# Bringing the tokens of experts 1 to 7 into columns with VectorE squares and SBUF transfers instead of TensorE turns

## The chip, the cores and the metric

The kernel runs on one core of one Trainium2 chip. The metric is the device time of one execution in microseconds (us); the median of three runs is given. Times taken from a trace are those of one profiled execution, counted from the start of its span.

Five engines work side by side, each in the order of its own instructions: TensorE (PE; its weight loads are PEld), VectorE (DVE), ScalarE (ACT), GpSimd (POOL) and SyncE (SP). They wait for each other by semaphores. In this kernel SP issues nearly all plain transfers, and POOL issues the indirect ones (gathers and scatters by an index).

## The reference: what is computed

Threshold attention over 8 batches, 8 heads, 576 positions and head size 64, and then a mixture of 8 experts over the 4608 resulting tokens of width 512. Each token goes to one expert, chosen by its id.

```python
scores = scale * np.matmul(q, k.transpose(0, 1, 3, 2))
thresh = np.max(scores, axis=-1, keepdims=True) - tau
scores = np.where(scores >= thresh, scores, -1000000000.0)
...
attn = np.exp(scores)
attn = attn / (np.sum(attn, axis=-1, keepdims=True) + 1e-09)
return np.matmul(attn, v).astype(np.float32)
...
x = np.ascontiguousarray(attn_out.transpose(0, 2, 1, 3)).reshape(B * S, H * D)
...
expert_idx = token_ids * np.int64(2654435761) % np.int64(E)
for e in range(E):
    mask = expert_idx == e
    ...
    xe = x[mask]
    h = np.maximum(xe @ w1[e], 0.0)
    out[mask] = h @ w2[e]
```

All is float32; w1 is 512 x 1024 and w2 1024 x 512 for each expert. With the inputs of the reference the experts get 598, 596, 571, 565, 599, 533, 570 and 576 tokens.

## The kernel before, in words

**Attention.** Two heads of one batch make a pair; there are 32 pairs, and the head pair `hp` is the outer loop (8 batches for each of the 4 head pairs). A pair takes 5 steps, and the loop `for n in range(LAST + NS + 1)` (L608) is an order written out by hand: within `tc.manual_schedule()` every engine gets its instructions in the order of the text. A step makes scores (`score`, L214), negates them and takes the row maximum (`negate`, L225, on VectorE), takes exponentials (`expo`, L239, on ScalarE), masks (`mask`, L250, on VectorE, with the threshold `thr` that GpSimd computes in L232), turns the weights (`turn_w`, L261) and multiplies by v (`av_part`, L292). At the end of a pair `put_xm` (L326) scales the result (`xm`, L331, on VectorE) and SP writes it to DRAM (L337, L342). Head pairs 0 to 2 go to `xa_dram`, 384 wide, head pair 3 to `xb_dram`, 128 wide (`x_place`, L313).

**Routing.** Small VectorE operations between the steps (`route`, L345) give every token a slot: expert e has the slots e x CAP to e x CAP + CAP - 1. CAP is 610: three tiles of 128 rows and two of 113. Tokens beyond CAP go to overflow slots, which the loop at the end (L805) would process; with these counts it makes no pass. Then `scatters` (L475) sends token numbers into two tables in DRAM by 36 indirect transfers, SP reads the tables back as `gidx` and `gidx_odd` (L488, four transfers), and VectorE takes their minimum (L494).

**Gathers.** `fetch(e, kt, part)` (L109) brings the 128 rows of tile `kt` of expert `e` from `xa_dram` (part 0) or `xb_dram` (part 1) into one of ten buffers `xg_bufs`. Part 0 of experts 0 and 1 is fetched in ten steps from step G0 = 130 on, part 1 after the attention loop (L698), when the last `xb_dram` write has landed.

**Expert 0** gets its columns early: `early_xT` (L539) turns blocks of 64 x 128 on TensorE and ScalarE copies them into `xT_0`. `early_h` (L561) multiplies head pairs 0 to 2 by w1 as filler between the last attention steps, and `late_h` (L576) adds head pair 3 and applies the maximum with 0.

**Experts** (L781, also in an order by hand): for each `e`, `gemm1` (L726: 8 blocks of hidden units, 2 halves of CAP/2 columns, 4 blocks of the width; not for expert 0), the load of w1 and the ten fetches for expert e + 2, `gemm2_last` (L749) for the last two tiles together, then for the first three tiles `gemm2` (L742), with `turn_last` (L764) turning the outputs of the last two tiles back. `store` (L771) copies to SBUF on ScalarE and scatters rows to `out` on POOL. Between these stand the pieces of `turn_x` for expert e + 1: `put_xT` (L719) makes four TensorE turns of 128 x 128 for each of five tiles (L722, against the identity matrix), and VectorE copies the result from PSUM into `xT` (L724).

Of the kernel before, what the change touches and what calls it, by code (L numbers as in the profile page):

```python
# [9 lines left out]
FP32 = mybir.dt.float32  # L10
BF16 = mybir.dt.bfloat16
FP16 = mybir.dt.float16
I32 = mybir.dt.int32
# [7 lines left out]
def kernel(  # L21
# [33 lines left out]

    KT, KF, TL = 5, 3, 113
    TROWS = [P] * KF + [TL] * (KT - KF)
    FIRST = [sum(TROWS[:k]) for k in range(KT)]
    CAP = sum(TROWS)
    CH = CAP // 2  # L60
# [4 lines left out]
               for m in range(1, E + 1) if m * (CAP + 1) <= N)  # L65

    slot_dram = [nc.dram_tensor(f"slot_scratch_{i}", (NSLOT, 1), I32, kind="Internal").ap()  # L70
                 for i in range(2)]

    XA = DIN - P
    xa_dram = nc.dram_tensor("xa_scratch", (N, XA), FP32, kind="Internal").ap()
    xb_dram = nc.dram_tensor("xb_scratch", (N, P), FP32, kind="Internal").ap()

# [14 lines left out]
    keep_any = consts.tile([P, 1], FP32, name="keep_any")  # L91
    drop = consts.tile([P, 1], FP32, name="drop")
    gidx = consts.tile([P, E, KT], I32, name="gidx")
    gidx_odd = consts.tile([P, E, KT], I32, name="gidx_odd")
    ov_i = consts.tile([P, NOV + 1], I32, name="ov_i")


    xg_bufs = [consts.tile([P, DIN], FP32, name=f"xg_{i}") for i in range(2 * KT)]
    xT_0 = consts.tile([P, CO, CAP], FP32, name="xT_0")
    h_0 = consts.tile([P, FO, CAP], FP32, name="h_0")  # L100
    w_tiles = {}

    def gather(x_dram, dst, idx):
        nc.gpsimd.indirect_dma_start(
            out=dst, out_offset=None, in_=x_dram[:, :],
            in_offset=bass.IndirectOffsetOnAxis(ap=idx, axis=0),
            bounds_check=N - 1, oob_is_err=False)

    def fetch(e, kt, part):  # L109
        xg = xg_bufs[(e * KT + kt) % (2 * KT)]  # L110
        dram, dst = (xa_dram, xg[:, 0:XA]) if part == 0 else (xb_dram, xg[:, XA:DIN])
        gather(dram, dst, gidx[:, e, kt:kt + 1])

# [10 lines left out]
    with tc.tile_pool(name="a_q", bufs=1) as a_q, \  # L124
# [188 lines left out]
        def x_place(p):  # L313
            hp, b = divmod(p, B)
            return (xa_dram, b * S, hp * P) if hp < HP - 1 else (xb_dram, b * S, 0)

# [9 lines left out]
        def put_xm(p):  # L326
# [8 lines left out]
                .to_broadcast([P, NS, 2, D]), op=ALU.mult)  # L335
            x_dram, r0, c0 = x_place(p)
            nc.sync.dma_start(  # L337
# [134 lines left out]

        placed = []

        def scatters():  # L475

            for c in range(NTC):
                nc.gpsimd.indirect_dma_start(
                    out=slot_dram[c % 2][:, :],
                    out_offset=bass.IndirectOffsetOnAxis(ap=slot_i[:, c:c + 1], axis=0),  # L480
                    in_=tok[:, c:c + 1], in_offset=None, bounds_check=NSLOT - 1,
                    oob_is_err=False)
                yield
            for _ in range(4):
                yield
            for table, dst in zip(slot_dram, (gidx, gidx_odd)):
                for p0, p1, k in ((0, TL, KT), (TL, P, KF)):
                    nc.sync.dma_start(  # L488
                        out=dst[p0:p1, :, 0:k],
                        in_=bass.AP(tensor=table.tensor, offset=p0 * KT,  # L490
                                    ap=[[k, p1 - p0], [CAP, E], [1, k]]))
            for _ in range(4):
                yield
            nc.vector.tensor_tensor(out=gidx[:], in0=gidx[:], in1=gidx_odd[:], op=ALU.min)  # L494

# [30 lines left out]
        def constants():  # L526
# [6 lines left out]
            nc.gpsimd.memset(gidx[:], BIG)  # L533
            nc.gpsimd.memset(gidx_odd[:], BIG)
            nc.gpsimd.iota(tok[:], pattern=[[1, NTC]], base=0, channel_multiplier=NTC)
# [3 lines left out]
        def early_xT(tr, k0, k1, c0, c1):  # L539

            blocks = [(kt, co) for kt in range(k0, k1) for co in range(c0, c1)]
            for i, (kt, co) in enumerate(blocks):
                for r in (0, 64):
# [3 lines left out]
                                        ident[r:r1, r:r1])  # L547
            for ka, kb in ((k0, min(k1, KF)), (max(k0, KF), k1)):
                for r in (0, 64):
# [41 lines left out]
        LAST = NS * NP  # L591
        G0 = NS * ((HP - 1) * B + 2)
        pieces, scatter_pieces = route(), scatters()
        h_pieces = early_h()

# [4 lines left out]
        with tc.manual_schedule():  # L600
# [7 lines left out]
            for n in range(LAST + NS + 1):  # L608
# [11 lines left out]
                if s == 3 and n < LAST:  # L620
                    next(pieces, None)
                if s == 1 and 3 <= p < 2 + len(xg_bufs):
                    nc.sync.dma_start(out=xg_bufs[p - 2][:], in_=xg_bufs[0][:])
                q = p - 1
                if s == 1 and 0 <= q < NP:
# [66 lines left out]

                g = n - G0
                if 0 <= g < 2 * KT:
                    fetch(g // KT, g % KT, 0)
                if n == LAST:
                    fill(1)
            for g in range(2 * KT):  # L698
                fetch(g // KT, g % KT, 1)
            fill(FO * 2 * (CO - 1) - 18)  # L700
            tr = ps_tr.tile([P, 2, 512], FP32, name="tr")
            early_xT(tr, 0, KT, CO - 1, CO)
            fill(18)
            late_h()

    with tc.tile_pool(name="m_x", bufs=1) as m_x, \
# [6 lines left out]

        o_bufs = [m_o.tile([P, DIN], FP32, name=f"o_{i}") for i in range(KT)]
        oT_sb = m_o.tile([P, CO, CAP - FIRST[KF]], FP32, name="oT_sb")
        for o_sb in o_bufs:
# [47 lines left out]
        def turn_last(kt, idx):  # L764
            o_ps = ps_x.tile([P, CO, P], FP32, name="xT_ps")
            s0 = FIRST[kt] - FIRST[KF]
            for co in range(CO):
                nc.tensor.transpose(o_ps[0:TL, co, :], oT_sb[:, co, s0:s0 + TL], ident[:])
            store(o_ps[:].rearrange("p c d -> p (c d)"), kt, idx, TL)

# [6 lines left out]

        def turn_x(e, kt):
            put_xT(xg_bufs[(e * KT + kt) % (2 * KT)], xT_bufs[e % 2], kt, TROWS[kt])

        with tc.manual_schedule():  # L781
            for e in range(E):
                if e > 0:
                    gemm1(w_tiles.pop((e, 1)), xT_bufs[e % 2], h_bufs[e % 2], 2, CH)
                if e + 2 < E:
                    load_w1(e + 2)
                    for g in range(2 * KT):
                        fetch(e + 2, g // 2, g % 2)
                w2_sb = w_tiles.pop((e, 2))
                if e + 1 < E:  # L790
                    turn_x(e + 1, 0)
                    turn_x(e + 1, 1)
                gemm2_last(w2_sb, h_bufs[e % 2])
                for kt in range(KF):
                    if e + 1 < E:
                        turn_x(e + 1, kt + 2)
                    gemm2(w2_sb, h_bufs[e % 2], kt, gidx[:, e, kt:kt + 1], P)
                    if kt < KT - KF:
                        turn_last(KF + kt, gidx[:, e, KF + kt:KF + kt + 1])
                if e + 2 < E:  # L800
                    load_w2(e + 2)
# [3 lines left out]
        with tc.For_i(0, n_ov, 1) as it:  # L805
# [14 lines left out]
            nc.vector.tensor_tensor(out=idx[:], in0=idx[:], in1=idx_odd[:], op=ALU.min)  # L820
            gather(xa_dram, xg_bufs[0][:, 0:XA], idx[:, 0:1])
            gather(xb_dram, xg_bufs[0][:, XA:DIN], idx[:, 0:1])
            put_xT(xg_bufs[0], xT_0, 0, P)
# [36 lines left out]
```

## Time and profile before

| what | us |
|---|---|
| median of three runs | 1042.09 (1041.54 to 1042.26) |
| profiled execution | 1026.92 |
| its span | 1025.3 |
| mean granted TensorE clock | 0.996 |
| w x v, L292, TensorE busy | 184.0 |
| gemm1, L731, TensorE busy | 231.2 |
| gemm2, L745, TensorE busy | 168.9 |
| gemm2_last, L757, TensorE busy | 99.0 |
| thresholds, L232, POOL busy | 102.3 |
| 40 + 40 gathers, L104, POOL busy | 43.8 + 40.3 |

A line of groups names the source line, the engine and the operation, what is written and read, the shape, how often, then the busy time and the mean duration of one, and last how long the engine sat idle before it and what ended that idle time. Matmul ends are modelled and overlap the next matmul's start by a little, so two starts are a better measure of a stage than a sum of durations. A product in float32 appears as two records. A timeline line begins with a start and a duration. "SPq" is the issuing of a transfer by SP.

### The profile page before, as it was taken

How to read it: one execution, taken by the hardware profiler on the slowest of the kernel's cores; microseconds unless marked ns; L12 is line 12 of the kernel's file. 1: busy time of each engine (PE TensorE's matmuls, PEld its weight loads, DVE VectorE, ACT ScalarE, POOL GpSimd, SP SyncE). 2: the span in 40 equal slices, each digit the busy share in tenths (PEclk: the TensorE clock that was granted, in tenths of full speed). 3: DMA queues.
4: the chain of work that ended last, by engine and by line, in shares of the span. 5: the costliest groups of instructions: out<-in, count | busy, mean ns of one | idle time of the engine just before them, and what ended most of it. 6: DMA issues, size and time to landing. Idle time of an engine off the chain costs nothing. (4 is left out here: it accounts for less than half of the span.)

```text
span 1025.3 us, 20443 instructions
## 1 busy us (share of the span) xinstructions
PE 1007.2 (98%) x7752; PEld 672.2 (66%) x7752; DVE 507.1 (49%) x1353; ACT 451.8 (44%) x737; POOL 316.4 (31%) x431
## 2 busy tenths in 40 slices
PE   8999999999999999999999999999999999999995
PEld 4666666666666666666857757668577577685772
DVE  7999999999999999983300101001001010010000
ACT  5888888888888988880210010000100100101001
POOL 3233332677773356322413041050140310101001
PEclk9999999999999999999999999999999999999998
DMA  7345554445565598311313241142042412300001
GB/s 178 84 113 138 137 123 114 94 111 118 118 186 155 141 250 197 82 33 27 131 42 133 82 154 43 81 153 82 35 139 82 143 40 93 108 1 37 10 1 47
DMA packets 92146, 103.50 MB, mean 101 GB/s; under 512 B 24709, under 2 KB 65788, under 8 KB 92048
## 3 DMA queue, kind: packets, MB, share of 16 engines
q1 hardware_dynamic: 83424, 83.06, 29.9%
q0 software_dynamic: 8192, 18.91, 5.5%
q8 instruction: 63, 1.03, 0.4%
q14 instruction: 35, 0.29, 0.1%
q10 hardware_dynamic: 432, 0.21, 0.1%
HBM read 81.87 MB, written 20.01 MB: 99 GB/s over the span
## 5 line engine op out<-in xcount | busy, mean ns | idle before, releaser
L239 ACT ACTIVATE w<-ns,nmx 128x576 f32<-128x576 f32 x288 | 220.3, 776 | 34.7 <-DVE ns L225 34.6
L731 PE MATMUL sc<-xT,w_sb 128*128 128x305 f32 x896 | 231.2, 419 | 0.0
L250 DVE SCALAR_TENSOR_TENSOR w<-ns,thr,w 128x576 f32<-128x576 f32 x288 | 226.0, 817 | 0.0
L731 PEld LDWEIGHTS sc<-xT,w_sb 128*128 128x128 f32 x896 | 169.3, 189 | 63.2 <-issue 3.3
L225 DVE TENSOR_SCALAR_CACHE_REDUCE ns<-sc 128x576 f32<-128x576 f32 x288 | 205.4, 746 | 6.2 <-PE sc L214 5.5
L214 PE MATMUL sc<-k_sb,q 64*128 64x288 f32 (+1 forms) x1280 | 178.9, 423 | 1.3 <-DVE k_sb L523 0.7
L745 PE MATMUL o_ps<-w_sb,h 128*128 128x512 f32 x384 | 168.9, 593 | 0.0
L774 POOL DMA_INDIRECT out_dram<-o,gidx x40 | 39.5, 987 | 409.0 <-ACT o L773 350.8
L261 PEld LDWEIGHTS tr<-ident,w 64*128 64x128 f32 x2624 | 107.0, 139 | 88.7 <-ACT wT_b L282 26.3
L232 POOL TENSOR_SCALAR thr<-nmx,drop 128x2 f32<-128x2 f32 (+1 forms) x160 | 102.3, 639 | 188.6 <-DVE ns L225 176.6
L739 DVE TENSOR_SCALAR h<-sc 128x610 f32<-128x610 f32 x28 | 22.2, 794 | 257.3 <-PE sc L731 257.3
L261 PE MATMUL tr<-ident,w 64*128 64x64 f32 x2624 | 139.4, 231 | 2.5 <-ACT wT_a L282 2.0
L745 PEld LDWEIGHTS o_ps<-w_sb,h 128*128 128x128 f32 x384 | 71.3, 190 | 80.3 <-issue 80.3
L724 DVE COPY xT<-xT_ps 128x512 f32<-128x512 f32 (+1 forms) x35 | 22.6, 662 | 179.3 <-PE xT_ps L722 179.3
L214 PEld LDWEIGHTS sc<-k_sb,q 64*128 64x128 f32 (+1 forms) x1280 | 93.2, 177 | 23.2 <-DVE ns L225 9.3
L292 PE MATMUL av<-wT_a,v 128*64 128x320 f32 (+1 forms) x704 | 100.8, 419 | 0.0
L737 ACT ACTIVATE h<-sc 128x610 f32<-128x610 f32 x28 | 19.0, 679 | 182.7 <-PE sc L731 182.7
L757 PE MATMUL sc<-h,w_sb 128*128 128x226 f32 x512 | 99.0, 353 | 0.0
L757 PEld LDWEIGHTS sc<-h,w_sb 128*128 128x128 f32 x512 | 96.2, 189 | 1.1
L282 ACT COPY wT_a<-tr 128x512 f32<-128x512 f32 (+1 forms) x128 | 81.7, 638 | 20.1 <-PE tr L261 19.6
L282 ACT COPY wT_b<-tr 128x512 f32<-128x512 f32 (+1 forms) x128 | 81.2, 635 | 9.3 <-PE tr L261 6.9
L292 PE MATMUL av<-wT_b,v 128*64 128x256 f32 x640 | 83.2, 389 | 0.0
(105 smaller groups left out, 607.4 us busy)
## 6 DMA issues: line engine op xcount, KB each, us to landing
w_sb<-in_moe_w_dram SPq DMA_DIRECT2D x16, 2048.0 KB
q<-in_q_dram SPq DMA_DIRECT2D x62, 288.0 KB
v<-in_v_dram SPq DMA_DIRECT2D x32, 256.0 KB
xa_scratch<-xm SPq DMA_DIRECT2D x24, 256.0 KB
k_sb<-in_k_dram SPq DMA_DIRECT2D x31, 144.0 KB
k_sb<-in_k_dram SPq DMA_DIRECT2D x32, 112.0 KB
xg<-xg SPq DMA_DIRECT2D x9, 256.0 KB
xb_scratch<-xm SPq DMA_DIRECT2D x8, 256.0 KB
```

What stands on the lines that cost most here:

```text
L214: nc.tensor.matmul(sc[out_rows, i, 0:S2], lhsT=q_sb[rows, h, q0:q1], rhs=k_sb[rows, h], start=True, stop=True)
L225: nc.vector.tensor_scalar(out=ns[:].rearrange("p (i s) -> p i s", i=2), in0=sc[:, :, 0:S2], scalar1=-1.0, scalar2=None, op0=ALU.mult, op1= ...
L232: nc.gpsimd.tensor_scalar(out=thr[:, 0:j + 1], in0=stats[n][0][:, 0:j + 1], scalar1=drop[:], scalar2=None, op0=ALU.add)
L239: nc.scalar.activation(w, nss[n, j][:], AF.Exp, bias=stats[n][0][:, j:j + 1], scale=-1.0)
L250: nc.vector.scalar_tensor_tensor(out=w, in0=nss.pop((n, j))[:], scalar=stats[n][1][:, j:j + 1], in1=w, op0=ALU.is_le, op1=ALU.mult, accum_ ...
L261: nc.tensor.transpose(dst[:, r, 64 * c:64 * c + 64], src[rows, c0:c0 + P], ident[rows, rows])
L282: nc.scalar.copy(dst, tr[:, :, 0:64 * n_c].rearrange("p r (c q) -> p r c q", c=n_c))
L292: nc.tensor.matmul(av[64 * j:64 * j + 64, g, c0:c1], lhsT=v_sb[:, c, 64 * j:64 * j + 64], rhs=wT[g][:, i, c0:c1], start=(c == 0), stop=stop)
L731: nc.tensor.matmul(h_ps[:, i, 0:width], lhsT=w1_sb[:, co, fo * P:fo * P + P], rhs=xT[:, co, i * width:i * width + width], start=(co == 0), ...
L745: nc.tensor.matmul(o_ps[0:rows], lhsT=h_sb[:, fo, FIRST[kt]:FIRST[kt] + rows], rhs=w2_sb[:, fo, :], start=(fo == 0), stop=(fo == FO - 1))
L757: nc.tensor.matmul(oT_ps[:, i, c * width:c * width + width], lhsT=w2_sb[:, fo, co * P:co * P + P], rhs=h_sb[:, fo, FIRST[KF]:CAP], start=( ...
L774: nc.gpsimd.indirect_dma_start(out=out[:, :], out_offset=bass.IndirectOffsetOnAxis(ap=idx, axis=0), in_=o_sb[:], in_offset=None, bounds_ch ...
```

## The change

CAP becomes 608 = 32 x 19, in tiles of 128, 128, 128, 128 and 96 rows. The two DRAM tensors for x become one, `x_dram`, with the view `x_rows` in which one head pair of one token is a row. Its last 128 columns are first filled with zeros by nine SP transfers in pairs 7 to 15; of the nine transfers that zeroed gather buffers four remain.

The slot tables are read into `stok`, 32 partitions by 19 slots for each expert, four times over (eight SP transfers); small VectorE copies make three index tiles from it: `gidx` (for the stores, and for expert 0), `gidx_0` (rows of `x_rows`, expert 0) and `gidx_x` (experts 1 to 7, in an order of slots in which the 32 x 32 squares end up side by side).

Expert 0 is gathered by head pairs: 15 gathers of 128 columns within attention, three in each of five pairs, and five after it. It goes through `early_xT` as before. Experts 1 to 7 are gathered by whole rows, five gathers each, into two sets of five buffers. `turn_x` then lets VectorE turn all 32 x 32 squares of a buffer in one instruction, five in all, into `xq`, and 16 SP transfers within SBUF bring 32 partitions x 4 x 160 (or 128) elements to the partitions where `xT` needs them. The TensorE turns L722 and the copies L724 are gone for these experts.

In the written order, `fill(18)` and `late_h` move behind the opening of the second group of buffers (whose set `xh` is filled with zeros), and `fetch(1)`, `fetch(2)` follow them. In the loop `turn_x(e + 1)` stands first, before `gemm1` of expert e; `fetch(e + 2)` stands where the ten fetches stood.

```diff
-    KT, KF, TL = 5, 3, 113
-    TROWS = [P] * KF + [TL] * (KT - KF)
-    FIRST = [sum(TROWS[:k]) for k in range(KT)]
-    CAP = sum(TROWS)
+    KT, KF, NB = 5, 3, 19
+    CAP = 32 * NB
+    FIRST = [P * k for k in range(KT)]
+    TROWS = [P] * (KT - 1) + [CAP - FIRST[-1]]
...
-    xa_dram = nc.dram_tensor("xa_scratch", (N, XA), FP32, kind="Internal").ap()
-    xb_dram = nc.dram_tensor("xb_scratch", (N, P), FP32, kind="Internal").ap()
+    x_dram = nc.dram_tensor("x_scratch", (N, DIN), FP32, kind="Internal").ap()
+    x_rows = x_dram.rearrange("n (h d) -> (n h) d", h=HP)
...
+    def fetch_0(kt, hp):
+        gather(x_rows, xg_bufs[kt][:, P * hp:P * hp + P], gidx_0[:, kt, hp:hp + 1])
...
-            for table, dst in zip(slot_dram, (gidx, gidx_odd)):
-                for p0, p1, k in ((0, TL, KT), (TL, P, KF)):
+            for table, dst in zip(slot_dram, (stok, stok_odd)):
+                for h in range(HP):
                     nc.sync.dma_start(
-                        out=dst[p0:p1, :, 0:k],
-                        in_=bass.AP(tensor=table.tensor, offset=p0 * KT,
-                                    ap=[[k, p1 - p0], [CAP, E], [1, k]]))
+                        out=dst[32 * h:32 * h + 32],
+                        in_=table[0:E * CAP].rearrange("(e c s) o -> c e (s o)", e=E, c=32))
             for _ in range(4):
                 yield
-            nc.vector.tensor_tensor(out=gidx[:], in0=gidx[:], in1=gidx_odd[:], op=ALU.min)
+            nc.vector.tensor_tensor(out=stok[:], in0=stok[:], in1=stok_odd[:], op=ALU.min)
+            yield
+            by_tiles(0, 1)
+            yield
+            for h in range(HP):
+                nc.vector.tensor_scalar(out=gidx_0[:, :, h], in0=gidx[:, 0], scalar1=float(HP),
+                                        scalar2=float(h), op0=ALU.mult, op1=ALU.add)
+                if h == 1:
+                    yield
+            routed.append(True)
+
+        def by_tiles(e0, e1):
+            for h in range(4):
+                rows, n = slice(32 * h, 32 * h + 32), (NB - h + 3) // 4
+                nc.vector.tensor_copy(gidx[rows, e0:e1, 0:n], stok[rows, e0:e1, h::4])
...
+        early = [(kt, hp) for kt in range(KT) for hp in range(HP - 1)]
...
-                if s == 1 and 3 <= p < 2 + len(xg_bufs):
+                if s == 1 and 3 <= p < 2 + KT:
                     nc.sync.dma_start(out=xg_bufs[p - 2][:], in_=xg_bufs[0][:])
+
+                if s == 1 and 2 + KT <= p < 2 + KT + N // DIN:
+                    r0 = DIN * (p - 2 - KT)
+                    nc.sync.dma_start(
+                        out=x_dram[r0:r0 + DIN, DIN - P:].rearrange("(t p) m -> p t m", p=P),
+                        in_=xg_bufs[0][:].rearrange("p (t m) -> p t m", m=P))
...
-                g = n - G0
-                if 0 <= g < 2 * KT:
-                    fetch(g // KT, g % KT, 0)
+                if n >= G0 and s > 1 and early:
+                    assert routed
+                    fetch_0(*early.pop(0))
                 if n == LAST:
                     fill(1)
-            for g in range(2 * KT):
-                fetch(g // KT, g % KT, 1)
+            assert not early
+            by_tiles(1, E)
+            for g in range(4):
+                rows, n = slice(32 * g, 32 * g + 32), min(KT, NB - KT * g)
+                nc.vector.tensor_copy(gidx_x[rows, 1:, 0:n], stok[rows, 1:, KT * g:KT * g + n])
+            for kt in range(KT):
+                fetch_0(kt, HP - 1)
             fill(FO * 2 * (CO - 1) - 18)
             tr = ps_tr.tile([P, 2, 512], FP32, name="tr")
             early_xT(tr, 0, KT, CO - 1, CO)
-            fill(18)
-            late_h()
...
-        def turn_x(e, kt):
-            put_xT(xg_bufs[(e * KT + kt) % (2 * KT)], xT_bufs[e % 2], kt, TROWS[kt])
+        def fetch(e):
+            for k in range(KT):
+                gather(x_dram, xg_sets[e % 2][k][:], gidx_x[:, e, k:k + 1])
+
+        def turn_x(e):
+            for k in range(KT):
+                nc.vector.transpose(out=xq[:, :, 32 * k:32 * k + 32],
+                                    in_=xg_sets[e % 2][k][:].rearrange("p (d a) -> p d a", a=32))
+            for g in range(4):
+                s0, s1 = 32 * KT * g, min(32 * KT * (g + 1), CAP)
+                for r in range(4):
+                    nc.sync.dma_start(out=xT_bufs[e % 2][32 * r:32 * r + 32, :, s0:s1],
+                                      in_=xq[32 * g:32 * g + 32, r::4, 0:s1 - s0])
 
         with tc.manual_schedule():
+            fill(18)
+            late_h()
+            fetch(1)
+            fetch(2)
             for e in range(E):
+                if e + 1 < E:
+                    turn_x(e + 1)
                 if e > 0:
                     gemm1(w_tiles.pop((e, 1)), xT_bufs[e % 2], h_bufs[e % 2], 2, CH)
                 if e + 2 < E:
                     load_w1(e + 2)
-                    for g in range(2 * KT):
-                        fetch(e + 2, g // 2, g % 2)
+                    if e > 0:
+                        fetch(e + 2)
                 w2_sb = w_tiles.pop((e, 2))
-                if e + 1 < E:
-                    turn_x(e + 1, 0)
-                    turn_x(e + 1, 1)
                 gemm2_last(w2_sb, h_bufs[e % 2])
                 for kt in range(KF):
-                    if e + 1 < E:
-                        turn_x(e + 1, kt + 2)
                     gemm2(w2_sb, h_bufs[e % 2], kt, gidx[:, e, kt:kt + 1], P)
```

## The prediction

> **What bounds the kernel now.** I read the page's busy rows first, then the stages, then the TensorE timeline of the last two experts, then the groups.
>
> ```profile
> span 1025.3 us, 20443 instructions
> PE 1007.2 (98%) x7752; PEld 672.2 (66%) x7752; DVE 507.1 (49%) x1353; ACT 451.8 (44%) x737; POOL 316.4 (31%) x431
> DVE  7999999999999999983300101001001010010000
> ...
> L722 PE MATMUL xT_ps<-ident,xg 128*128 128x128 f32 (+1 forms) x140 | 19.2, 267 | 0.0
> L724 DVE COPY xT<-xT_ps 128x512 f32<-128x512 f32 (+1 forms) x35 | 22.6, 662 | 179.3 <-PE xT_ps L722 179.3
> ```
>
> The first rows show a kernel in two halves. Until slice 17 (about 455 us) VectorE is full as well as TensorE: that is attention. After that VectorE has almost nothing to do and TensorE alone is full: that is the experts. L722, the turning of gathered tokens on TensorE, has no idle before it, so it lies on the engine that sets the end. L724 waits 179.3 us for TensorE: VectorE there is free. What L722 costs is read from the timeline of experts 6 and 7 (start, duration), because expert 7 has no successor to turn:
>
> ```profile
> 879.41 33.03 PE L731 MATMUL sc<-xT,w_sb 128*128 128x305 f32 x128
> 912.28 1.03 PE L722 MATMUL xT_ps<-ident,xg 128*128 128x128 f32 x8
> 913.15 12.38 PE L757 MATMUL sc<-h,w_sb 128*128 128x226 f32 x64
> ...
> 948.09 33.03 PE L731 MATMUL sc<-xT,w_sb 128*128 128x305 f32 x128
> 980.96 12.38 PE L757 MATMUL sc<-h,w_sb 128*128 128x226 f32 x64
> 993.17 7.03 PE L745 MATMUL o_ps<-w_sb,h 128*128 128x512 f32 x16
> ...
> 1007.78 7.03 PE L745 MATMUL o_ps<-w_sb,h 128*128 128x512 f32 x16
> ```
>
> Expert 6 lasts from 879.41 to 948.09, 68.68 us. Expert 7 runs from 948.09 with no gap; its last L745 would be followed at 1007.78 + 6.88 (the pitch 948.09 - 941.21 of the same group before) = 1014.66, so 66.57 us. The difference, **2.11 us**, is the real price of one expert's turning, and expert 7 is a picture of what every expert becomes.
>
> **Part 1, removed from TensorE.** Experts 1 to 7: 7 x 2.11 = **-14.8 us**. The L722 row says 19.2 us because modelled ends overlap the next group (912.28 + 1.03 is past 913.15); starts decide. Nothing new becomes late on TensorE: expert 7 shows gemm2_last starting right behind gemm1.
>
> **Part 2, narrower.** CAP goes from 610 to 608 (the fullest expert has 599 tokens, so no overflow pass either way). L731's pitch is 32.87/64 = 514 ns for 305 columns, 1.68 ns each: one column less in 64 products is 0.11 us, in seven experts and in expert 0's early and late halves 0.9 us. L757 loses two columns in 32 products, 0.11 us x 8 = 0.9. Together **-1.7 us** (12.2 us/(32 x 226) gives the same 1.7 ns a column). turn_last keeps four 128-column turns; only its row counts change. The ACT copies of early_xT fall from 8 to 6 before the first fills (6 of L559 in 1.69 us): **-0.3**, between 0 and -0.6.
>
> **Part 3, the new way of the tokens.** Per expert: 5 whole-row gathers instead of 10, 5 VectorE turns, 16 SP transfers. POOL saves 5 x 1.3 us of issue, off the path. A VectorE turn has no row; its ends are a MEMSET of 128x512 (485 ns) and L724 (662 ns); I take 662, so 3.3 us an expert. The SP transfers inside SBUF have one neighbour, L623 xg<-xg, 0.59 us to issue; landing I take from the last token write, whose issue ends at 475.68 and which releases the gather at 477.77: 2.1 us. So 16 x 0.6 + 2.1 = 11.7 us. Cover:
> - Expert 1 is tightest. Gathers for it start behind expert 0's five (477.77 + 5 x 1.31 = 484.3), the last lands near 494. VectorE reaches the turns after late_h's last add (500.41 + 0.79 = 501.2), ends at 504.5, transfers land at 516.2. gemm1(1), before at 536.02, starts 2.11 + 0.1 earlier: 533.8. Spare: 17.6 us. Queued on SP behind the transfers is load_w1(2), needed some 70 us later.
> - Later experts: gathers issue behind the previous stores, early in gemm1(e-1); the turns stand behind its relus on VectorE; the transfers behind load_w2(e) on SP, at the start of the next expert, with one expert (66 us) to land. VectorE is busy 6.3 us in 70. Behind the waiting turns stand the relus of gemm1(e): the turns' inputs landed an expert earlier. Cost 0, and up to 6 us if transfers ran singly.
>
> **Rules against it.** The Trainium skill (VectorE: DVE Perf Modes, "The three transpose paths" and its rules) says a 128x128 turn belongs on TensorE when PSUM will do: 390 ns there, 311 ns on VectorE and in 32x32 blocks only. By 390 the removal would be worth 140 x 0.39 = 55 us; the trace has 2.11/20 = 106 ns a turn, so the trace's 14.8 stands. The advice weighs one engine against another; here one is full, the other idle. And DMA: Bandwidth & Descriptors ("Anatomy of one DMA") gives about 2.0 us fixed per DMA of GpSimd's kind: 16 of 80 KB one after another would be 16 x 2.2 = 35 us (an estimate), landing at 539.7, 5.9 us late for expert 1. SP's timeline shows transfers issued every 0.6 us while earlier ones fly, so I keep 11.7.
>
> **Part 4, attention pays.** VectorE is the bound there: pairs (starts of xm, L331) come every 13.90 us, and the pair holding the one index minimum takes 14.07:
>
> ```profile
> 330.40 0.82 DVE L331 TENSOR_TENSOR xm<-av,rec 128x640 f32<-128x640 f32 x1
> ...
> 340.52 0.19 DVE L494 TENSOR_TENSOR gidx<-gidx,gidx_odd 128x40 int32<-128x40 int32 x1
> ...
> 344.47 0.82 DVE L331 TENSOR_TENSOR xm<-av,rec 128x640 f32<-128x640 f32 x1
> ```
>
> So 0.17 us a small operation. Added: four copies, four multiply-adds (8 x 0.15 = 1.2) and a minimum 152 wide instead of 40 (+0.1): **+1.3 us**. The other eight index copies and five more memsets come near 474, with VectorE idle 1 to 2 us between L572 copies: 0.
>
> The index table's loads: SP is caught behind a 2 MB weight load,
>
> ```profile
> 320.44 0.59 SPq L121 DMA_DIRECT2D w_sb<-in_moe_w_dram  x1
> 321.21 12.04 SPq L488 DMA_DIRECT2D gidx<-slot_scratch  x2
> 333.43 5.61 SPq L488 DMA_DIRECT2D gidx_odd<-slot_scratch  x2
> 339.16 0.66 SPq L170 DMA_DIRECT2D k_sb<-in_k_dram  x1
> ```
>
> and is free only 1.4 us before the minimum reads them at 340.52. The change makes eight loads of 32 x 8 pieces: 2048 pieces, as before (2 x 128 x 8), in twice as many transfers. Ends: 0 if pieces set the time, +18 if transfers do. The 120-piece load waited longest, behind the 904-piece one, so pieces (and the weights) set it: **+0.5** (0 to 2).
>
> Gathers during attention: 15 instead of 10, in three steps of five. Ten in a row (372 to 400 us) left pairs at 13.91 and 13.90. New is one x tensor for all four head pairs: a gather now waits for the last token write and the next write waits for it. The write issued at 392.45 to 394.04 lands at 396.1; POOL wants to gather at 393.2, and the threshold behind it, due at 395.2, would end at 398.1, against a mask due at 397.9: **+0.3** (0 to 2).
>
> Zero-filling transfers, 13 against 9, lie on SP early in attention, with loads two pairs ahead: 0.
>
> **Sum:** -14.8 - 1.7 - 0.3 + 1.3 + 0.5 + 0.3 = -14.7. The profiled execution took 1026.92 (1.6 around its span), giving 1012.2. The runs' median, 1042.09, lies 15.2 above the profiled one; I carry that over: **1027.4 us**.
>
> **Rivals.**
> 1. *The busy column is right.* L722 frees 19.2: 1023.0. Against it: the 2.11 repeats in every expert. 5%.
> 2. *Attention stalls more.* Table loads and gather waits at their upper ends, 2 + 2 and VectorE's extras at 2: 1031 to 1036. For it: only 1.4 us of margin at 340.52. 10%.
> 3. *Expert 1 waits for its tokens*, transfers one at a time: 1027.4 + 5.9 = 1033.3. 4%.
> 4. *Slower.* SP's table loads cost by the transfer: 17.95 us for four is 4.5 each, 36 for eight, so the minimum comes about 18 us late, and VectorE, in order, holds all of attention: 1027.4 + 18 = 1045. It decides from 14.7 us of stall. 4%.
> 5. A change that does nothing would need L722's time to come back as gaps; expert 7 has none. 1%.
>
> **Numbers.** 76% for the forecast (1025 to 1030), the rest as above. Faster by over 0.2% (2.1 us, about what a measurement can tell): 0.93; within: 0.02; slower: 0.05. Range 1024.6 to 1031.5: the unknown costs at their lower ends plus a little of rival 1, and up to the foot of rival 2.
>
> **What would show it.** Expert pitch near 66.4 (right if L731 starts that far apart); no L731 idle at expert 1; the pair at 330 to 345 longer by 1 to 2 us; a DVE idle released by a slot_scratch load means rivals 2 or 4. It is wrong if TensorE idles at the start of any gemm1.

## The result, and the profile after

The changed kernel takes **1022.82 us** (median of four runs, 1022.60 to 1024.54) against 1041.95 us for the kernel before in the same set: ratio 0.982, 95% interval 0.9803 to 0.9837. The gain is 19.1 us where 14.7 were forecast. The profiled execution took 1024.54 us, so here it lies above the median, not 15 us under it.

The page of the changed kernel, and below it its TensorE timeline of experts 6 and 7 (start, duration):

```profile
span 1022.9 us, 20290 instructions
## 1 busy us (share of the span) xinstructions
PE 998.9 (98%) x7612; PEld 660.4 (65%) x7612; DVE 511.1 (50%) x1374; ACT 452.1 (44%) x735; POOL 287.8 (28%) x406
...
DVE  7999999999999999994240200100101001000000
```

```profile
882.00 32.91 PE L760 MATMUL sc<-xT,w_sb 128*128 128x304 f32 x128
914.75 12.27 PE L786 MATMUL sc<-h,w_sb 128*128 128x224 f32 x64
...
948.33 32.91 PE L760 MATMUL sc<-xT,w_sb 128*128 128x304 f32 x128
```

TensorE still fills the experts, and the turns of tokens are gone from between its products: gemm2_last follows gemm1 at once, and an expert lasts 948.33 - 882.00 = 66.33 us instead of 68.68. That part is as forecast. What is not is the hand-over from attention to the experts. The timeline of the same execution, TensorE, VectorE and GpSimd (the end of a line names the idle time before it and what ended it):

```profile
499.82 1.29 PE L597 MATMUL sc<-xT,w_sb 128*128 128x304 f32 x4 [0.28 <-ACT xT L574]
507.09 5.30 PE L597 MATMUL sc<-xT,w_sb 128*128 128x304 f32 x12 [5.97 <-DVE h L587]
...
506.24 0.79 DVE L587 COPY h<-sc 128x608 f32<-128x608 f32 x1 [9.76 <-remote]
...
504.06 1.01 POOL L108 DMA_INDIRECT xg<-x_scratch,gidx_x  x1 [0.31 <-issue]
```

TensorE stands still for 5.97 us because one VectorE copy comes late. The products that the copy reads end at about 500 by the trace; the copy starts 2.2 us after GpSimd begins to issue the last of 15 gathers in a row. "remote" is a releaser that this view can't name; the section on e12 to e14 comes back to it.

### The profile page after: what moved, and what is told of

It is laid out like the page before. It is cut to its first block, busy times and chain, and to the rows that moved or that the text cites. A ratio compares the mean times of both kernels' runs of the same rounds, so it can differ in the third digit from the quotient of the medians.

```text
span 1022.9 us, 20290 instructions
## 1 busy us (share of the span) xinstructions
PE 998.9 (98%) x7612; PEld 660.4 (65%) x7612; DVE 511.1 (50%) x1374; ACT 452.1 (44%) x735; POOL 287.8 (28%) x406
## 5 line engine op out<-in xcount | busy, mean ns | idle before, releaser
L760 PE MATMUL sc<-xT,w_sb 128*128 128x304 f32 x896 | 230.4, 419 | 0.0
L768 DVE TENSOR_SCALAR h<-sc 128x608 f32<-128x608 f32 x28 | 22.2, 792 | 408.2 <-PE sc L760 370.2
L766 ACT ACTIVATE h<-sc 128x608 f32<-128x608 f32 x28 | 19.0, 677 | 182.0 <-PE sc L760 182.0
L786 PE MATMUL sc<-h,w_sb 128*128 128x224 f32 x512 | 98.2, 353 | 0.0
L802 ACT COPY o<-o_ps 128x512 f32<-128x512 f32 x24 | 14.0, 585 | 147.0 <-issue 87.3
```

The costliest lines, as they stand in the source:

```text
L760: nc.tensor.matmul(h_ps[:, i, 0:width], lhsT=w1_sb[:, co, fo * P:fo * P + P], rhs=xT[:, co, i * width:i * width + width], start=(co == 0), ...
L786: nc.tensor.matmul(oT_ps[:, i, c * width:c * width + width], lhsT=w2_sb[:, fo, co * P:co * P + P], rhs=h_sb[:, fo, FIRST[KF]:CAP], start=( ...
```

## Experiments

The runs of one set share a chip, and each set has the kernel before in it. The sets fall into two kinds: in five sets, and in the profile on which the forecast was built, the kernel before takes 1026 to 1027 us; in three sets, and in the plain times beside the forecast and the result, 1042 to 1045 us. Below they are the **1026 sets** and the **1043 sets** (the expectations call them chips of the quicker and of the slower kind). Why a set is of one kind was not found. The number of the chip doesn't settle it: number 1 stands with a set of each kind. Pairs are counted from one start of `xm` to the next, from 1 to 31.

| run | kind | median | ratio to before, 95% interval |
|---|---|---|---|
| e1 before | 1026 | 1026.02 | 0.9994 (0.9985 to 1.0003) |
| e2 changed | 1026 | 1010.73 | 0.9846 (0.9830 to 0.9863) |
| e3 before, no turns | 1026 | 1010.66 | 0.9846 (0.9830 to 0.9862) |
| e4 before, CAP 608 | 1026 | 1024.25 | 0.9975 (0.9967 to 0.9982) |
| e5 way doubled | 1026 | 1038.10 | 1.0118 (1.0100 to 1.0137) |
| e9 gathers twice | 1026 | 1012.46 | 0.9865 (0.9848 to 0.9881) |
| e11 changed | 1043 | 1024.07 | 0.9815 (0.9799 to 0.9830) |
| e6 w2 later | 1043 | 1023.74 | 0.9815 (0.9799 to 0.9831) |
| e7 64 rows | 1043 | 1021.75 | 0.9796 (0.9780 to 0.9812) |
| e8 index on GpSimd | 1043 | 1022.71 | 0.9803 (0.9786 to 0.9820) |
| e12 before | 1026 | 1026.35 | 0.9998 (0.9990 to 1.0006) |
| e13 changed | 1026 | 1010.57 | 0.9837 (0.9824 to 0.9851) |
| e10 three repairs | 1026 | 1008.08 | 0.9814 (0.9801 to 0.9828) |
| e14 before | 1043 | 1042.89 | 0.9994 (0.9985 to 1.0002) |
| e15 fetch(2) later | 1026 | 1010.84 | 0.9834 (0.9820 to 0.9848) |
| e18 = e15 | 1043 | 1015.47 | 0.9731 (0.9707 to 0.9755) |
| e17 = e10 + e15 | 1026 | 1008.22 | 0.9821 (0.9807 to 0.9834) |
| e19 = e17 | 1026 | 1008.03 | 0.9818 (0.9800 to 0.9835) |

### e1, e2: both kernels again

No edit; two traces from one chip.

> The kernel before, unchanged, profiled anew, because its profiled execution (1026.92) lies 15.2 us under the median of its runs and the profile after does not (1024.54 against 1022.82). Theory A: the first profiled execution was a lucky one, free of stalls that the other executions have; then most executions, and a new profile, show about 1042 us, and the trace shows some 15 us of stalls at places where the first had none (the hand-over from attention to experts, 455 to 505 us, and the pairs of attention). Theory B: the time without a profile carries a constant 15 us more; then the new profile shows 1027 again and the runs 1042.

> The changed kernel, unchanged, profiled anew. Theory A: runs and profile both near 1023, with the 6 us wait for a late VectorE copy at 500 to 507 us and the lower clock at 463 to 467 us either there again or not; where they are absent, an execution near 1009 to 1013 is seen. Theory B: a profile near 1008 and runs near 1023.

Measured: 1026.02 and 1010.73, a gain of 15.8 us against the set's runs of before. Neither theory of e1 holds as it stands: before's plain runs are not 15 us above the profile here, but equal to it. This first put the 15.2 us in doubt.

### e3, e4: the two halves of the change alone, on the kernel before

e3 leaves out every `put_xT` of the expert loop: experts 1 to 7 multiply stale columns, so only its time is of use. e4 only makes tiles narrower.

```diff
# e3, from before.py
+        nc.vector.memset(xT_bufs[1][:], 0.0)
-                if e + 1 < E:
-                    turn_x(e + 1, 0)
-                    turn_x(e + 1, 1)
...
-                    if e + 1 < E:
-                        turn_x(e + 1, kt + 2)
# e4, from before.py
-    KT, KF, TL = 5, 3, 113
+    KT, KF, TL = 5, 3, 112
```

> The kernel before with the 140 TensorE turns of experts 1 to 7 and their copies left out (the experts then multiply stale columns; gathers, CAP 610 and everything else stay). Theory: the turns cost their pitch, 7 x 2.11 = 14.8 us, so 14.8 us less than before, and every expert 66.57 us long. Rival: the busy column is right, 19.2 us less. If the end of the execution (from the last scatter to the end of the span, 8.6 us before, 5.9 us after) depends on the turns, it shortens here too; if on the gathers, it stays.

> The kernel before with CAP 608 (tiles of 128, 128, 128, 112, 112) and nothing else. Theory: 1.7 us less than before, from one column less in 64 products of each expert and two less in 32. Rival: 608 columns cost the same as 610, no difference.

Measured: e3's experts all lie 66.56 us apart, 2.12 under before's 68.68, so the turns cost 7 x 2.12 = 14.8 us by the pitch (16.07 by the medians). The busy column's 19.2 is refuted. e4 gains 2.5 us by the medians; its pitch is 68.44, and against e12 its trace is 1.8 us shorter between the last `xm` and the last scatter, where 1.7 were expected, and 0.4 in attention. Both parts together are more than the whole change gains on these chips (15.8): something is paid back.

### e5: is the new way hidden?

Three VectorE turns for each one, and every SBUF transfer issued twice.

```diff
-            for k in range(KT):
+            for k in [k for k in range(KT) for _ in range(3)]:
...
-                for r in range(4):
+                for r in (0, 0, 1, 1, 2, 2, 3, 3):
```

> The changed kernel with every VectorE turn done three times and every one of the 16 transfers done twice. Theory: the new way lies wholly beside TensorE, so no difference to the changed kernel (within 0.5 us), and no gemm1 starts late. Rival: it is covered only just; then each expert is longer by part of 6.8 us of turns or 12 us of transfers, 10 us or more in all.

First the way as it is, in e13's timeline of VectorE, SP and TensorE:

```profile
504.15 3.08 DVE L815 STREAM_TRANSPOSE xq<-xh 128x512 f32<-128x512 f32 x5
520.24 3.08 DVE L815 STREAM_TRANSPOSE xq<-xg 128x512 f32<-128x512 f32 x5 [13.01 <-DMA xT<-xq]
...
507.37 11.12 SPq L820 DMA_DIRECT2D xT<-xq  x16
...
536.90 3.49 PE L760 MATMUL sc<-xT,w_sb 128*128 128x304 f32 x13
```

Five turns take 3.08 us. The next turns, for expert 2, need `xq` free and so show when the 16 transfers have landed: 520.24, 12.9 us after the first was issued. gemm1 of expert 1 starts at 536.90: 16.7 us to spare. Then e5, TensorE and SP; the expectation, no difference, failed:

```profile
538.66 3.12 PE L760 MATMUL sc<-xT,w_sb 128*128 128x304 f32 x8 [3.11 <-DMA xT<-xq]
564.12 32.49 PE L760 MATMUL sc<-xT,w_sb 128*128 128x304 f32 x120 [22.33 <-DMA xT<-xq]
630.03 32.91 PE L760 MATMUL sc<-xT,w_sb 128*128 128x304 f32 x128
...
513.32 49.18 SPq L820 DMA_DIRECT2D xT<-xq  x32
```

The second transfer of each pair writes where the first did and waits for it, so the issuing of 32 transfers takes 49.2 us, 3.07 a pair. Expert 1 waits 3.11 + 22.33 = 25.4 us, which is nearly all of the 27.4 us that e5 is slower than e2 (the changed kernel of another 1026 set). No later expert waits: from expert 2 on (630.03) they stay 66.33 apart. The cover is about as wide as forecast, and in e5 it runs out at expert 1 alone. It is there because transfers overlap: sixteen of 3.07 us each would be 49 us (an estimate), 36 more than the 12.9 seen. Rival 3's mechanism is real and was only not met.

### e9: what a gather costs, and the end of the kernel

```diff
-            for k in range(KT):
+            for k in [k for k in range(KT) for _ in range(2 if e > 2 else 1)]:
```

> The changed kernel with the whole-row gathers of experts 3 to 7 issued twice, which makes 156 indirect transfers, as many as before (131 in the changed kernel). Theory: the end of the execution grew shorter with the number of GpSimd's transfers, whose queue is drained last; then it is back at 8.6 us (the closing drain of GpSimd 4.2 us instead of 2.1) and the time is 2.5 us above the changed kernel. Rival: it depends on something else, and the end stays at 5.9 us.

Measured 1.8 us slower than the changed kernel of the other 1026 sets (2.5 was expected), with nothing late in the experts. The time is at the very end. The last scatter, by GpSimd's timelines of e12 (before), e13 (changed) and e9:

```profile
1016.58 0.98 POOL L774 DMA_INDIRECT out_dram<-o,gidx  x1 [2.88 <-ACTq L805]
```

```profile
1002.32 0.98 POOL L803 DMA_INDIRECT out_dram<-o,gidx  x1 [2.89 <-ACTq L848]
```

```profile
1000.96 0.98 POOL L803 DMA_INDIRECT out_dram<-o,gidx  x1 [2.83 <-ACTq L848]
```

The spans end at 1026.0, 1009.3 and 1010.3: 9.4, 7.0 and 9.3 us after that start. Before and e9 issue 156 indirect transfers in all, the changed kernel 131. So 25 transfers fewer shorten the close of the kernel by 2.4 us, though they are gathers that were needed long before; e9 puts 25 back and nearly all of the 2.4 us return. e3, which drops the turns and keeps the 156 transfers, closes in 8.7 us, so it is not the turns. Over all traces the close takes 8.7 to 9.6 us with 156 and 6.7 to 7.4 with 131. Nothing of this was in the forecast.

### e11, e6, e7, e8, e10: what attention pays, and three repairs

e11 is the changed kernel. e7 turns 64 rows for the last tile too; e8 gives the eight small index operations to GpSimd; e6 loads the second w2 five pairs later; e10 is all three.

```diff
# e7
-                    r1 = min(r + 64, TROWS[kt])
+                    r1 = r + 64
# e8
-                nc.vector.tensor_scalar(out=gidx_0[:, :, h], in0=gidx[:, 0], scalar1=float(HP),
+                nc.gpsimd.tensor_scalar(out=gidx_0[:, :, h], in0=gidx[:, 0], scalar1=float(HP),
...
-                nc.vector.tensor_copy(gidx[rows, e0:e1, 0:n], stok[rows, e0:e1, h::4])
+                (nc.vector if e0 else nc.gpsimd).tensor_copy(gidx[rows, e0:e1, 0:n], stok[rows, e0:e1, h::4])
# e6
-                if s == 2 and p in (22, 26):
-                    load_w2((p - 22) // 4)
+                if s == 2 and p in (22, 31):
+                    load_w2((p - 22) // 9)
```

> The changed kernel once more, beside the three next runs on the same chip. Theory: 15 to 17 us under the kernel before, on whatever chip the two are timed together; the profile again shows experts of 66.33 us. If this chip is one on which the kernel before takes about 1042 us, its trace shows whether the hand-over again holds waits that other chips do not show.

> The changed kernel with the lower block of tile 4 turned as 64 rows instead of 32 in early_xT (the rows beyond 96 are zeros and are not copied). Theory: the six turns of that tile took 1.20 us instead of 0.40 because 64-row and 32-row turns alternate on TensorE; with 64 rows they take 0.40 again, and the time falls by 0.8 to 1.0 us. Rival: the 0.8 us are a wait for ScalarE's copies, which are wider now; then nothing changes.

> The changed kernel with the eight small index operations of expert 0 moved from VectorE to GpSimd. Theory: they stretch pairs 22 and 23 on the full VectorE (14.83 and 14.05 us instead of 14.06 and 13.91); on GpSimd, which is a third busy, pair 22 returns to about 14.2 and the time falls by 0.7 us. Rival: GpSimd's thresholds come late behind them and the mask waits; then no gain, or a loss.

> The changed kernel with w2 of expert 1 loaded in pair 31 instead of pair 26. Theory: the stretched pair (15.03 us instead of 13.90) comes from a gather that waits for a token write caught behind this load; with the load gone from there no pair from 24 to 30 is longer than 13.95, and the time is up to 1.1 us less than the changed kernel's. Rival: the wait is the gather's on its own (one x tensor), and a pair stays stretched. Loading later could also make expert 1 wait for w2; its gemm2_last comes some 75 us after the load, so no.

> Three small repairs of the changed kernel at once: turns of 64 rows for the last tile of expert 0, the eight index operations on GpSimd, and the second w2 load five pairs later. If the 0.8 us of pair 31 and the 0.8 us of pair 22 add up, this is 1.6 us under e13; with the 1.1 us of pair 26, if the weight load was its cause, 2.7. If the gains of attention are swallowed at the hand-over, it equals e13 within 0.5 us.

e11 gains 18.6 us on before where 15 to 17 was expected on any chip: the gain depends on the kind of set.

The early columns of expert 0, last six turns, by TensorE's timelines of e13 (changed), e7 and e12 (before):

```profile
457.40 1.20 PE L560 MATMUL sc<-ident,xg 64*128 64x64 f32 x6 [0.91 <-ACT xT L574]
```

```profile
461.61 0.40 PE L560 MATMUL sc<-ident,xg 64*128 64x64 f32 x6 [0.91 <-ACT xT L574]
```

```profile
457.69 0.40 PE L545 MATMUL sc<-ident,xg 64*128 64x64 f32 x6 [0.92 <-ACT xT L559]
```

The last tile has 96 rows, so turns of 64 and of 32 rows alternate, and six of them take 1.20 us; all of 64 rows, more work, take 0.40. That heights alternate is not enough for the loss: before's last tile has 113 rows, its turns alternate between 64 and 49, and they take 0.40 too. Why 32 rows cost more is open. The 0.8 us lie on the path: pair 31 is 17.84 us long in e7 and 18.63 in e11. By the medians e7 gains 2.3, more than this explains.

The index work, in VectorE's timeline of e13:

```profile
340.20 0.31 DVE L495 TENSOR_TENSOR stok<-stok,stok_odd 128x152 int32<-128x152 int32 x1
...
343.41 0.68 DVE L509 COPY gidx<-stok 32x5 int32<-32x5 int32 x4
...
347.14 0.24 DVE L500 TENSOR_SCALAR gidx<-gidx 128x5 int32<-128x5 int32 x2
```

The pair with the minimum is 14.83 us here and 14.07 in e12, the next 14.05 and 13.90: 0.9 us paid. With e8 they are 14.05 and 13.89, so the work is free on GpSimd (1.4 us by the medians). e6 changes nothing that can be told apart, 0.33 us, and its pairs 26 and 28 last 14.49 and 14.69 us where none was to pass 13.95; in a 1043 set, where such pairs are stretched anyway, that decides nothing.

The gathers in pair 26 sometimes cost what the forecast feared. e2's timeline, GpSimd, VectorE and SP, and one line of the list of SP's waits (us in total, times, longest):

```profile
397.50 1.10 POOL L108 DMA_INDIRECT xg<-x_scratch,gidx  x1 [4.68 <-DVE ns L227]
...
398.97 0.82 DVE L252 SCALAR_TENSOR_TENSOR w<-ns,thr,w 128x576 f32<-128x576 f32 x1 [1.10 <-POOL thr L234]
...
393.58 0.37 SPq L339 DMA_DIRECT2D x_scratch<-xm  x1
...
SPq L339 <- DMA xg<-x_scratch,gidx: 1.7, 1, 1.7
```

The write of x waits for the gathers of the pair before and goes out 7.5 us after its `xm` starts (5.3 in e13), the next gather waits for the write, the threshold queues behind the gather, and VectorE waits 1.10 us for the threshold. (The line of the gather names a VectorE instruction long past; it waited for the write.) Why those gathers land late is open: SP was also held up to 391.75 by a load of v, but in e5, stalled too, that load ends at 389.65 and the wait for the gathers is 2.7 us. The pair takes 15.03 us there, 15.38 in e5, and 13.89 in e13, e9 and e15: a stall that some executions have.

e10 takes 1008.08, 2.5 us under e13 on the same chip, about the 2.7 expected. Its pair 31 is 17.84 against e13's 20.27, but 1.65 of that difference is no repair: e2's is 18.62, and in e13 TensorE's granted clock falls to 0.94 and 0.89 between 450 and 470 us. So 1.7 us (0.8 there, 0.9 of index work) are shown by stages, and the share of the later load is open: e13 has no stall in pair 26 that it could take away.

### e12 to e14: where the kernel before loses 15 us

> The kernel before, unchanged, for a trace beside e13's on the same chip. If the chip is of the kind on which before takes 1042 us: the theory that the forecast failed by carrying 15.2 us over as a constant expects the loss in stages that both kernels share, pairs of attention stretched by 0.3 to 0.9 us and the hand-over from attention to the experts longer than 62.8 us, with the pitch of the experts still 68.7 us. The rival, that the change itself gains more there, expects a pitch above 70 us. On a chip of the other kind: 1026.6 us, and the question stays open.

> The changed kernel beside e12. Either 1010.7 us (15.9 under e12) or 1023 to 1024 us (18 to 19 under e12). The pitch of the experts is 66.3 us in both cases; where the gain is 3 us larger, the theory looks for it in the hand-over or in attention pairs, not in the experts.

> The kernel before once more, for its trace. On a chip of the slower kind (1042 us): a hand-over longer than 62.8 us, stretched pairs of attention, and a pitch of the experts of 68.7 us by the theory, above 70 us by the rival. On the other kind 1026.6 us, and nothing new.

e12 fell into a 1026 set, e14 into a 1043 set. With e11 the four traces give, in us:

| stage | before, 1026 (e12) | changed, 1026 (e13) | before, 1043 (e14) | changed, 1043 (e11) | e18, 1043 |
|---|---|---|---|---|---|
| first to last `xm` | 437.63 | 440.84 | 441.90 | 444.52 | 444.03 |
| last `xm` to gemm1(1) | 62.75 | 60.67 | 76.92 | 68.85 | 61.09 |
| gemm1(1) to last scatter | 479.73 | 465.42 | 479.73 | 465.42 | 465.43 |
| last scatter to end | 9.4 | 7.0 | 9.4 | 7.3 | 7.3 |

The experts take the same in both kinds to 0.01 us. What a 1043 set adds to the kernel before is 4.3 us of attention and 14.2 us of hand-over. In attention only pairs that issue indirect transfers are longer: of pairs 11 to 20, 25 and 26, nine by 0.3 to 0.8 us and three not, and every other pair agrees with e12 within 0.02. The hand-over, in e14's timeline of TensorE, VectorE, ScalarE and GpSimd:

```profile
492.01 0.52 PE L545 MATMUL tr<-ident,xg 64*128 64x64 f32 x10
...
495.65 1.19 PE L582 MATMUL sc<-xT,w_sb 128*128 128x305 f32 x4
506.52 2.40 PE L582 MATMUL sc<-xT,w_sb 128*128 128x305 f32 x4 [9.68 <-DVE h L572]
...
505.68 0.79 DVE L572 COPY h<-sc 128x610 f32<-128x610 f32 x1 [12.76 <-remote]
...
494.92 0.98 ACT L559 COPY xT<-tr 128x192 f32<-128x192 f32 x4 [20.05 <-remote]
...
505.67 1.00 POOL L104 DMA_INDIRECT xg<-xb_scratch,gidx  x1 [0.30 <-remote]
```

It is the stall of the changed kernel, but 9.68 us long (and 1.17 more behind it): here 19 gathers follow attention in a row, not 15, and VectorE's copy starts when the last is issued. TensorE's granted clock is 0.53 from 500 to 507 us and 0.50 from 507 to 514, and the other 3.3 of the 14.2 us fall in this stretch. So the change shortens in a 1043 set a wait that a 1026 set doesn't have: the hand-over falls by 8.07 us there, and by 2.08 in a 1026 set.

What "remote" stands for can be read from the semaphore updates in the same traces. The copy waits for a counter that TensorE raises when products are done. The update that frees it comes at 505.65, 9.8 us after the modelled end of its product; in the profile of the result section it comes at 506.22, 6.7 us after. ScalarE is held in the same way: its copies (L559) start 2.4 us after the turns that they read (L545), in e12 0.05 us after. So it is not VectorE that is held, but the word from TensorE.

It is what sets the two kinds apart. The seven traces of 1043 sets have 28 to 40 updates of this counter that come over 0.15 us after the modelled end of any product, the thirteen of 1026 sets 0 to 2, none over 0.2 us (the first 30 and the last 25 us left out). Of these 221 late updates 219 stand beside an indirect transfer, where about a quarter of all its updates stand. The updates of VectorE, ScalarE and GpSimd are late in no trace. As the ends of products are modelled, it stays open whether the products or only their signals are late.

### e15, e17 to e19: is it the row of gathers?

If so, ten gathers in a row end before the copy is due.

```diff
             fetch(1)
-            fetch(2)
...
                     gemm2(w2_sb, h_bufs[e % 2], kt, gidx[:, e, kt:kt + 1], P)
+                    if e == 0 and kt == 0:
+                        fetch(2)
```

> The changed kernel, but the five gathers for expert 2 stand behind the first store of expert 0, so that ten instead of fifteen gathers follow attention without a pause. On a chip of the slower kind (before at 1042): if VectorE stands still until the queue of gathers ends, the queue ends 6.6 us earlier, the 5.8 to 6 us in which TensorE is idle at the hand-over go, and the time falls from 1023.5 to about 1018; by the rival, in which the stall has another cause, it stays at 1023 to 1024. On a chip of the quicker kind (before at 1026.6) there is no such stall, and it equals the changed kernel, 1010.6, within 0.5 us.

> The three repairs of e10 and the later gathers of e15 together. On a chip of the quicker kind 1008.1, as e10. On the slower kind: about 1015.5 if e15 brings 5.8 there, about 1021 if it brings nothing.

> e15's kernel again. On a chip of the slower kind 1018 if the stall of VectorE ends with the queue of gathers (10 instead of 15), 1023 to 1024 if it has another cause. On the quicker kind 1010.7.

> e17's kernel again. On a chip of the slower kind about 1013, if the repairs take 2.5 off e18's 1015.5 as they took 2.5 off the changed kernel elsewhere; 1015.5 if they bring nothing there. On the quicker kind 1008.2, as e17.

e15 met a 1026 set and equals the changed kernel there, as was expected there. e18, the same kernel in a 1043 set, takes 1015.47, lower than the 1018 expected. Its timeline:

```profile
500.47 7.80 PE L597 MATMUL sc<-xT,w_sb 128*128 128x304 f32 x28 [0.28 <-DVE h L587]
...
499.62 0.79 DVE L587 COPY h<-sc 128x608 f32<-128x608 f32 x1 [3.52 <-PE sc L583]
...
497.10 1.01 POOL L108 DMA_INDIRECT xh<-x_scratch,gidx_x  x1 [0.30 <-issue]
```

The last gather of the row is issued at 497.10, the copy waits for TensorE by name, TensorE's idle time falls from about 6 us to 0.28, and the hand-over takes 61.09 us, close to the 60.67 of a 1026 set. Late updates remain (28), but none is over 1.5 us. That the length of the stall hangs on the row of gathers is shown. How gathers delay what TensorE reports, and only in some sets, is not: earlier copies of the same line pass undisturbed while gathers are issued (three of e11's, each 3.07 us after the other). e17 and e19 take 1008.22 and 1008.03, both in 1026 sets, so this last version was not seen in a 1043 set. It beats both kernels where it was measured; e18 beats both in the other kind.

## Why the prediction was right and wrong

**Part 1, right.** 2.11 us an expert by starts: e3 shows 2.12, and the changed kernel 66.33 where 66.4 was named. Rivals 1 and 5 fall. The Trainium skill's 390 ns a turn (VectorE: DVE Perf Modes, "The three transpose paths"; given there for bf16) would have asked for 55 us; the 16 us that e3 gained have no room for it.

**Part 2, right.** The pitch falls by 2.35, so CAP brings 0.24 an expert, forecast 0.22. Gemm1(1) to last scatter, and the hand-over in the 1026 sets, fall by 14.3 + 2.1 = 16.4, forecast 16.5.

**Its last item, wrong in sign.** The -0.3 for the ACT copies of `early_xT` is +0.8. The copies did fall from eight to six and brought nothing (pair 31: 17.85 in e12, 17.84 in e7), but the turns that feed them now have 64 and 32 rows and take 1.20 us instead of 0.40. The diff showed 96 rows; "what is removed" was counted and the new shape of what stays was not.

**Part 3, right.** Turns of 3.08 us, forecast 3.3; landing after 12.9 us, forecast 11.7; spare at expert 1 16.7, forecast 17.6. By the estimate of 35 us from the Trainium skill's fixed cost of a DMA (DMA: Bandwidth & Descriptors, "Anatomy of one DMA") expert 1 would have been late; it was not, and e5 shows 3.07 us a pair once transfers do wait for each other. Rival 3 falls by this.

**Part 4, right in kind.** Index work 0.9 where 1.3 and, for the table loads, 0.5 stood; no VectorE wait for the table showed, so rivals 2 and 4 fall. The coupling of gathers and writes, forecast 0.3, is nothing in some executions and 1.1 to 1.5 in others, by the chain that was described. Attention as a whole pays 2.7 us (e1 to e2), with the early turns, where 1.8 was forecast.

**Left out: the end.** 2.4 us less between the last scatter and the end of the span, with 25 indirect transfers fewer. The forecast counted the fewer gathers as "off the path".

In the 1026 sets these terms make -16.4 + 2.7 - 2.4 = -16.1 where -14.7 was forecast and the medians show -15.8. That the sum came so close is in part luck, for two misses work against each other: attention paid 0.9 more than forecast, and the close, put at nothing, gave 2.4.

**The step that failed** is the last of the sum: "The runs' median, 1042.09, lies 15.2 above the profiled one; I carry that over". The 15.2 us were not an offset between profiled and plain executions. Profile and times belong to two kinds of sets, and what lies between these is time in two stages of the kernel, by e14 against e12 4.3 us in attention and 14.2 at the hand-over (before the first `xm`, e14 is 0.9 us quicker). The change shortens the second, because 15 gathers follow attention instead of 19. Why a set is of one kind stays open. What is left of it is 1022.82 - 1010.65 (the mean of e2 and e13) = 12.2 us in the changed kernel, and 1015.47 - 1010.84 = 4.6 in e15's. Of the miss of 4.6 us, 3.0 come from this and 1.6 from the sum of the parts: 1012.2 forecast for what takes 1010.65. The gap of 1.5% between 1026.92 and 1042.09 stood in the table before the prediction, and the range should have reached down for the case that it shrinks.

## What to carry to other kernels

When a profiled time lies far from the median of the runs, don't carry the difference over: it sits in some stage, and the change may touch it; the range has to hold both cases. Indirect transfers cost in places where GpSimd's issue time shows nothing: at the end of the kernel (2.4 us for 25) and, in some sets, in what other engines wait for from TensorE while a row of them is issued, so count them, and keep long rows of them away from a hand-over. When a size changes, look at what the unchanged lines now do with it: 96 rows in place of 113 tripled the time of six turns.

## What the runs showed of the hardware that was not expected

- One kernel, 1026.6 us in some sets and 1043 in others, with the experts equal to 0.01 us and the difference beside indirect transfers: 4.3 us in attention, 14.2 at the hand-over.
- In 1043 sets TensorE's semaphore updates come late beside indirect transfers, 28 to 40 times a trace, by up to 11 us after the modelled end of a product (0 to 2 times and 0.2 us in 1026 sets). At the hand-over this leaves TensorE idle for 9.7, about 6 and 0.3 us with rows of 19, 15 and 10 gathers.
- The close of the kernel takes 9.4 us after the start of the last scatter with 156 indirect transfers and 7.0 with 131.
- TensorE turns of 64 and 32 rows, alternating, take 0.20 us each; of 64 rows alone, or of 64 and 49 alternating, 0.07.
